# More attention units along block 0, longer DRAM runs for v, k and q, a shorter warm-up, and the last expert's rows turned part by part

## The chip, the cores and the metric

The kernel runs on one core of a Trainium2 chip. The metric is the device time of one execution in microseconds; lower is better. The core's engines have names in the profile: PE (TensorE, matrix products; PEld are its weight loads), DVE (VectorE), ACT (ScalarE), POOL (GpSimd) and SP (SyncE, which issues most DMAs).

## The reference

Three stages follow each other. Inputs are 4 x 8 heads of 576 x 64 q, k and v, and weights.

```python
# 1. attention with random features, for each of 32 heads
phi(x) = exp(h - max(h)) / sqrt(m),  h = x @ omega.T - sum(x * x) / 2
kv = phi(k).T @ v;  z = sum(phi(k))
x = (phi(q) @ kv) / (phi(q) @ z + 1e-6)         # 2304 tokens x 512
# 2. a dense layer
h = x @ w_in                                    # 512 -> 2048
x = (h - tanh(h)) @ w_out                       # 2048 -> 512
# 3. eight experts; each token goes to one, 288 tokens to each
logits = x @ w_gate                             # best pairs (token, expert) first
out[tokens of e] = relu(x[tokens of e] @ w1[e]) @ w2[e]    # 512 -> 1024 -> 512
```

All values are float32. The kernel keeps that precision by splitting operands into a high and a low part and adding three products.

## The kernel before

**Attention** is cut into 72 units. A unit is two heads' worth of a granule of 256 tokens (or of a shared tile of 128). PE projects the granule (line 436, one group of matmuls for two units), DVE takes the negative maxima (`nm`, line 450), ACT the exponentials (`phi`, line 447). For k, PE then adds into `kv` (line 467); for q it transposes `phi` (line 489), multiplies by `kvs` (line 496), and DVE divides (`den`, `xt`, lines 515 to 509).

**The dense layer** runs over six blocks of 384 tokens. A block has 16 chunks of 128 hidden columns. A chunk's first product (`x @ w_in`, lines 611 to 613, twelve matmuls of 384 columns) goes through ACT and DVE (`s`, lines 615 to 638) to the high and low part `gH` and `gL`; its second product (line 658, nine matmuls of 512 columns) adds into three accumulators. Blocks 4 and 5 run together. The weights come in as 32 raw pieces and are prepared on the chip by `weight_ops`: DVE makes `wf` in three passes (lines 341, 343, 345), ACT the high part, DVE or POOL the low part (`lw`, `oL`), which is stored in DRAM and fetched again in each block. In blocks 1 to 3 DVE also multiplies `w_out` with the gate's rows (line 739).

**The experts** follow, one after another, each for 288 tokens in groups of 128, 128 and 32. Its last step multiplies into `py` for four slices d of 128 output columns, copies each to `yT`, transposes them to rows (line 1459), copies these to `mL`, and POOL scatters them (line 1463).

**The order** of the work is not written by hand. Each step is handed to a planner (`Plan`) with a due time `plan.at`, a cost for each engine that may do it, and the buffers that it reads and writes. The planner walks through the steps by its own account of the engines' times, gives each the engine that ends it first, and so fixes one order per engine before the kernel runs; on the chip each engine follows its list strictly. The numbers at the end of `tile_kernel` set the due times: the first 18 units come before block 0 (`NEARLY`), and `along` says how many of the other 54 are spread along each of the blocks 0 to 4:

```python
along = [16, 14, 14, 10, 0]
starts, steps = [T_MLP], []
due = [4.0 + T_UNIT * i for i in range(NEARLY)]
for j, n in enumerate(along):
    steps.append((SB * (1.6 if j == 4 else 1.0) + SU * n) / NF)
    starts.append(starts[j] + NF * steps[j])
    due += [starts[j] + DUE0 + i * (NF * steps[j] - DUE1) / max(n, 1) for i in range(n)]
```

Where the planner sees PE idle for long, it adds short products of ones (`spare`, line 1489) in the stages up to the last weight. The kernel opens with fifteen such products of 512 columns (`warm`, line 1480). In the program there is also a general branch for large values, which this input doesn't take.

## Time and profile before

| what | us |
|---|---|
| median of 3 runs | 867.41 |
| fastest and slowest of them | 864.65, 870.2 |
| the profiled execution | 868.87 |
| its span, from the first to the last instruction | 867.1 |

The page of the profile lists each engine's busy time in the span, and cuts the span in slices; the views behind it give the busy time of any stretch, the waits of an engine and its instructions in order of time. Matmuls overlap in their pipeline, so the distance from one start to the next tells more than the duration of one.

### The profile page before, as it was taken

To read this page: it belongs to the slowest core of one execution; us is meant where nothing else is said; L and a number is where in the kernel's file an instruction comes from. 1 tells how busy PE (TensorE), PEld (TensorE's weight loads), DVE (VectorE), ACT (ScalarE), POOL (GpSimd) and SP (SyncE) were. 2 spreads that over 40 slices of the span, in tenths; PEclk is the share of its full clock that TensorE was granted. 3 is DMA by queue.
4 is the path that set the end of the run, shared out by engine and by line. 5 is a ranking of instruction groups with operands and counts; after the bars stand their busy time and mean duration, and the time that the engine had idled before them with its cause. 6 is when DMAs were issued, how large, how long until landed. Compare 5 with 4: busy or idle time off the path is not lost. (4 is left out here: it accounts for less than half of the span.)

```text
span 867.1 us, 17421 instructions
## 1 busy us (share of the span) xinstructions
PE 839.3 (97%) x6126; PEld 750.9 (87%) x6126; DVE 651.8 (75%) x1906; ACT 470.5 (54%) x1024; POOL 272.5 (31%) x292
## 2 busy tenths in 40 slices
PE   7998999999999999999999999999999999999995
PEld 5988888898888888788988996777999999999995
DVE  6979999778777888878878867445878878876720
ACT  4966564655457554565558864013565555554721
POOL 2131343433353345344423334010042142142211
PEclk9989999999999999999999999999999999999998
DMA  8979877977557665743459884668879879779600
GB/s 258 337 261 286 275 250 236 313 257 241 147 178 226 189 207 161 233 141 113 122 191 320 290 300 144 186 219 267 250 221 299 249 211 301 250 193 343 225 28 28
DMA packets 103790, 193.95 MB, mean 224 GB/s; under 512 B 28305, under 2 KB 42257, under 8 KB 103698
## 3 DMA queue, kind: packets, MB, share of 16 engines
q1 hardware_dynamic: 97586, 172.80, 60.5%
q0 software_dynamic: 5664, 18.88, 9.0%
q8 instruction: 49, 0.80, 0.4%
q10 hardware_dynamic: 448, 1.11, 0.4%
q14 instruction: 43, 0.35, 0.1%
HBM read 149.64 MB, written 33.69 MB: 211 GB/s over the span
## 5 line engine op out<-in xcount | busy, mean ns | idle before, releaser
L305 POOL TENSOR_TENSOR gL<-s,gH 128x384 fp32r<-128x384 f32 x68 | 80.0, 1178 | 172.9 <-ACT gH L300 163.7
L611 PE MATMUL bk<-xH,wi 128*128 128x384 f32 x332 | 118.3, 356 | 4.6 <-ACT phi L447 2.7
L739 DVE SCALAR_TENSOR_TENSOR lw<-wf,raw 128x512 f32<-128x512 f32 x128 | 108.9, 850 | 5.3 <-POOL wf L736 2.6
L612 PE MATMUL bk<-xL,wi 128*128 128x384 f32 x332 | 112.1, 338 | 0.0
L613 PE MATMUL bk<-xH,iL 128*128 128x384 f32 x332 | 112.1, 338 | 0.0
L658 PE MATMUL acc<-wo,gL 128*128 128x512 f32 x282 | 111.4, 396 | 0.0
L658 PE MATMUL acc<-wo,gH 128*128 128x512 f32 x240 | 98.8, 412 | 0.0
L658 PE MATMUL acc<-oL,gH 128*128 128x512 f32 x240 | 95.1, 396 | 0.9 <-DVE oL L305 0.8
L447 ACT ACTIVATE phi<-bk,nm 128x128 f32<-128x128 f32 x268 | 75.8, 384 | 32.9 <-DVE nm L450 32.6
L736 POOL TENSOR_TENSOR wf<-oL,wo 128x512 f32<-128x512 f32 x48 | 66.7, 1390 | 38.7 <-DMA oL<-low_wo 36.3
L611 PEld LDWEIGHTS bk<-xH,wi 128*128 128x128 f32 x332 | 63.0, 190 | 11.9 <-ACT phi L447 3.4
L636 DVE SCALAR_TENSOR_TENSOR s<-s,bk 128x384 f32<-128x384 f32 x83 | 45.4, 549 | 33.2 <-ACT s L635 32.8
L615 ACT ACTIVATE s<-bk 128x384 f32<-128x384 f32 x80 | 39.2, 490 | 55.1 <-PE bk L613 49.2
L300 ACT ACTIVATE gH<-s 128x384 fp32r<-128x384 f32 x80 | 42.0, 525 | 46.2 <-DVE s L638 28.1
L612 PEld LDWEIGHTS bk<-xL,wi 128*128 128x128 f32 x332 | 63.1, 190 | 2.8
L658 PEld LDWEIGHTS acc<-wo,gL 128*128 128x128 f32 x282 | 52.9, 188 | 12.3 <-POOL gL L305 0.5
L613 PEld LDWEIGHTS bk<-xH,iL 128*128 128x128 f32 x332 | 62.9, 189 | 0.0
L638 DVE SCALAR_TENSOR_TENSOR s<-s,s 128x384 f32<-128x384 f32 x80 | 55.4, 693 | 0.9
L635 ACT ACTIVATE s<-s,qbias 128x384 f32<-128x384 f32 x80 | 49.3, 616 | 6.3 <-DVE gL L305 1.9
L658 PEld LDWEIGHTS acc<-oL,gH 128*128 128x128 f32 x240 | 45.2, 188 | 7.4 <-DVE oL L305 1.6
L658 PEld LDWEIGHTS acc<-wo,gH 128*128 128x128 f32 x240 | 45.2, 188 | 6.8 <-issue 1.0
L450 DVE TENSOR_REDUCE nm<-bk 128x4 f32<-128x512 f32 (+1 forms) x74 | 45.7, 633 | 6.8 <-PE bk L436 6.2
(413 smaller groups left out, 2320.4 us busy)
## 6 DMA issues: line engine op xcount, KB each, us to landing
r_wraw<-in_moe_w_dram SPq DMA_DIRECT2D x50, 512.0 KB, 5.3
iL<-low_wi SPq DMA_DIRECT2D x80, 256.0 KB, 3.2
oL<-low_wo SPq DMA_DIRECT2D x78, 256.0 KB, 3.1
raw<-in_moe_w_out_dram SPq DMA_DIRECT2D x32, 512.0 KB, 4.3
raw<-in_moe_w_in_dram SPq DMA_DIRECT2D x30, 512.0 KB, 5.2
s_wraw<-in_moe_w_dram SPq DMA_DIRECT2D x14, 512.0 KB, 5.8
dw<-in_moe_w_dram SPq DMA_DIRECT2D x13, 512.0 KB, 5.3
w1l<-dw SPq DMA_DIRECT2D x13, 512.0 KB, 3.0
```

The costliest lines, as they stand in the source:

```text
L305: (nc.gpsimd if e == POOL else nc.vector).tensor_tensor(out, in_, high.bitcast(F32), op=OP.subtract)
L447: nc.scalar.activation(ph.t[:, i0 + i, :], pj.t[:, i * M:(i + 1) * M], AF.Exp, bias=nmx.t[:, i0 + i:i0 + i + 1])
L450: plan.op(DVE, 0.1 + 0.125 * n, lambda e, pj=pj, i0=i0, n=n: V.tensor_reduce(nmx.t[:, i0:i0 + n], pj.t[:, :n * M].rearrange("p (i m) -> p ...
L611: nc.tensor.matmul(ph(), piece(iH, c), xH.t[:, c, :], start=(c == 0), stop=False)
L612: nc.tensor.matmul(ph(), piece(iH, c), xL.t[:, c, :], start=False, stop=False)
L613: nc.tensor.matmul(ph(), piece(iL, c), xH.t[:, c, :], start=False, stop=(c == NC - 1))
L635: plan.op(ACT, 0.52, lambda e: nc.scalar.activation(s.t, ut(), AF.Square, bias=qbias), r=[u], w=[s], lag=2.8)
L636: plan.op(DVE, 0.52, lambda e: V.scalar_tensor_tensor(s.t, s.t, QD, ph(), op0=OP.add, op1=OP.mult), r=[p, s], w=[s], lag=3.4)
L638: plan.op(DVE, 0.65, lambda e: V.scalar_tensor_tensor(s.t, s.t, QC, ut(), op0=OP.mult, op1=OP.mult), r=[u, s], w=[s], lag=4.0)
L658: nc.tensor.matmul(acc[t].t, (gL if k == 2 else gH).t[:, c], (oL if k == 1 else oH).t, start=(f == 0 and k == 0), stop=(f == end and k == ...
L736: plan.op(POOL, 1.45, lambda e: nc.gpsimd.tensor_tensor(w.t, lo.t.bitcast(F32), wo[:, f, :].bitcast(F32), op=OP.add), r=[lo, wbuf["wo", f] ...
L739: x_reads.append(plan.op(DVE, 0.9, lambda e, i=i: nc.vector.scalar_tensor_tensor(scratch.t.bitcast(F32), w.t, 1.0, half(rows[i // 2], i % ...
```

## The change

The number of units along blocks 0 to 3 becomes 25, 8, 11 and 10; still 54 in all. The times around them change as well: unit and weight due times, and how far ahead x and the low parts are asked for. The planner starts its engines at about a microsecond, takes 300 instead of 280 bytes per ns for DMA, and adds fillers for shorter gaps in the first 25 us. The host lays v out with its column of ones and in the order of the tiles, so that one DMA loads a granule in runs of 2 KB per partition (it was one or two DMAs in pieces of 64 floats, and a memset on POOL); k and q are laid out so that a granule is one run per partition. `omega` comes twice as tall from the host and takes one DMA. The two constants for ACT no longer hold up the projections. One raw weight instead of two is loaded over ACT's queue. The warm-up has seven products. For the last expert the slices are transposed as they come, into one bank for each group of tokens; the last slice is copied in three parts.

```diff
-        self.free = dict.fromkeys(("PE", "ACT", "DVE", "POOL", "SP", "-"), 0.0)
+        self.free = {"PE": 1.6, "ACT": 0.9, "DVE": 1.5, "POOL": 1.2, "SP": 0.9, "-": 0.0}
...
-            if e == "PE" and self.fill and t - self.free[e] > 0.9:
+            if e == "PE" and self.fill and t - self.free[e] > (0.5 if t < 25.0 else 0.9):
...
-                self.dma = max(self.dma, end) + o.nbytes / 280e3
+                self.dma = max(self.dma, end) + o.nbytes / 300e3
...
-        for i in range(2):
-            plan.op(ACT, 0.6, lambda e, i=i: nc.scalar.dma_start(omT[i * D:(i + 1) * D, :], omega), w=[bT], nbytes=P * D * 4)
+        plan.op(ACT, 0.6, lambda e: nc.scalar.dma_start(omT, omega), w=[bT], nbytes=P * M * 4)
...
-            plan.op(ACT, 0.8, lambda e, x=x: nc.scalar.activation(x, x, AF.Copy), w=[bT])
+            plan.op(ACT, 0.8, lambda e, x=x: nc.scalar.activation(x, x, AF.Copy), w=[bBias])
...
-        first = kind == "wi" and f < 2 and not masked
+        first = kind == "wi" and f < 1 and not masked
...
-            plan.op(POOL, 0.04, lambda e: nc.gpsimd.memset(t.t[:, :n, :, D:], 1.0), w=[t], lag=-6.0)
-            for i in range(n):
-                plan.op(SP, 0.47, lambda e, i=i: nc.sync.dma_start(
-                    t.t[:, i, :, :D], v[(tile + i) * P:(tile + i + 1) * P, hh * HH * D:(hh + 1) * HH * D].rearrange(
-                        "p (h d) -> p h d", d=D)), w=[t], lag=-5.0, nbytes=P * HH * D * 4)
+            W = HH * (D + 1)
+            plan.op(SP, 0.47, lambda e: nc.sync.dma_start(
+                t.t.rearrange("p i h d -> p (i h d)")[:, :n * W], v[b // 2, hh, :, tile % 9 * W:(tile % 9 + n) * W]),
+                w=[t], lag=-5.0, nbytes=P * W * 4 * n)
...
-            t.t[:, :, :n * P], src[nm][b // 2, hh * HH * D:(hh + 1) * HH * D, c0:c0 + n * P].rearrange(
-                "(a p) n -> p a n", p=P)), w=[t], lag=-6.0, nbytes=P * HH * D * 4 * n)
+            t.t.rearrange("p a n -> p (a n)")[:, :2 * n * P], src[nm][b // 2, hh, :, 2 * c0:2 * (c0 + n * P)]),
+            w=[t], lag=-6.0, nbytes=P * HH * D * 4 * n)
...
-    LAG2, LEADX, LEADI, LEADO = 10.35, 14.35, 8.14, 3.98
+    LAG2, LEADX, LEADI, LEADO = 10.35, 12.18, 8.65, 5.9
...
-                        plan.at = max(x_due[i * TPB + t] + 11.86, start[j - 1] + LEADX)
+                        plan.at = max(x_due[i * TPB + t] + 15.38, start[j - 1] + LEADX)
...
+    def end_rows(p, d, py, yT):
+
+        if not d:
+            tails[:] = [(Buf(bank3), Buf(mLr), []) for _ in range(NG)]
+        ends = d == NC - 1
+        cp = None
+        if not ends:
+            plan.op({ACT: 0.3, DVE: 0.37}, 0, lambda e: copy(e, yT.t, py.t[:, :CAP]), r=[py], w=[yT])
+            plan.at += 1.0
+        for g in range(NG):
+            (po, yo, done), n, ix = tails[g], GN[g], idxs[p][g][0]
+            cols = slice(g * GS, g * GS + n)
+            if ends:
+                cp = plan.op((ACT, DVE, ACT)[g], 0.2, lambda e, cols=cols: copy(e, yT.t[:, cols], py.t[:, cols]),
+                             r=[py], wp=[yT])
+            done.append(plan.op(PE, 0.11, lambda e, po=po, n=n, cols=cols: nc.tensor.transpose(
+                po.t[:n, d * P:(d + 1) * P], yT.t[:, cols], ident), rp=[yT], wp=[po],
+                after=([cp] if ends else [yT.writers[-1]]) + done[-1:]))
+            if d >= NC - 2:
+                part = slice(0, d * P + P) if not ends else slice(d * P, DM)
+                w = part.stop - part.start
+                plan.op((ACT, DVE, ACT)[g], 0.1 + 0.001 * w, lambda e, po=po, yo=yo, n=n, part=part: copy(
+                    e, yo.t[:n, part].bitcast(F32), po.t[:n, part]), rp=[po], wp=[yo], after=done[-1:])
+            if ends:
+                plan.op(POOL, 1.1, lambda e, g=g, yo=yo, ix=ix: scatter(g, yo, ix), r=[yo, ix], late=3.5)
...
+            if p == E - 1:
+                end_rows(p, d, py, yT)
+                continue
...
-        for i in range(15):
+        for i in range(7):
             nc.tensor.matmul(idle.t, onev.to_broadcast([P, P]), onev.to_broadcast([P, DM]), start=True, stop=True)
...
-    T_UNIT, T_MLP, DUE0, DUE1 = 2.23, 60.95, 7.39, 19.25
+    T_UNIT, T_MLP, DUE0, DUE1 = 2.31, 60.95, 7.04, 19.25
...
-    SB, SU = 39.84, 2.29
-    along = [16, 14, 14, 10, 0]
+    SB, SU = 39.84, 2.36
+    along = [25, 8, 11, 10, 0]
...
-    WI0, WI1, WO0 = 3.84, 2.4, -13.4
+    WI0, WI1, WO0 = 4.16, 1.93, -6.82
```

DVE at the start of the kernel, before: `wf` are passes over a raw weight, `nm` the maxima of a unit.

```order
L315 TENSOR_SCALAR omT<-omT 128x128
L341 TENSOR_SCALAR wf_215<-raw_187 128x512
L343 SCALAR_TENSOR_TENSOR wf_215<-raw_187,wf_215 128x512
L450 TENSOR_REDUCE nm_230<-bk_205 128x4
L450 TENSOR_REDUCE nm_232<-bk_206 128x4
L345 SCALAR_TENSOR_TENSOR wf_215<-raw_187,wf_215 128x512
```

The same place now:

```order
L315 TENSOR_SCALAR omT<-omT 128x128
L451 TENSOR_REDUCE nm_201<-bk_191 128x4
L451 TENSOR_REDUCE nm_205<-bk_192 128x4
L341 TENSOR_SCALAR wf_212<-raw_164 128x512
L343 SCALAR_TENSOR_TENSOR wf_212<-raw_164,wf_212 128x512
L345 SCALAR_TENSOR_TENSOR wf_212<-raw_164,wf_212 128x512
```

The first two maxima moved ahead of the first weight.

DVE in the middle of block 0, before, from the ninth chunk's polynomial (the `s` that reads a bank `bk`) on:

```order
L636 SCALAR_TENSOR_TENSOR s_1467<-s_1467,bk_1360 128x384
L343 SCALAR_TENSOR_TENSOR wf_1475<-raw_1394,wf_1475 128x512
L638 SCALAR_TENSOR_TENSOR s_1467<-s_1467,s_1462 128x384
L345 SCALAR_TENSOR_TENSOR wf_1475<-raw_1394,wf_1475 128x512
L450 TENSOR_REDUCE nm_1519<-bk_1486 128x4
L636 SCALAR_TENSOR_TENSOR s_1512<-s_1512,bk_1416 128x384
```

Now, from the ninth chunk on:

```order
L637 SCALAR_TENSOR_TENSOR s_1454<-s_1454,bk_1402 128x384
L305 TENSOR_TENSOR gL_1475<-s_1184,gH_1464 128x384
L341 TENSOR_SCALAR wf_1486<-raw_1357 128x512
L639 SCALAR_TENSOR_TENSOR s_1454<-s_1454,s_1444 128x384
L343 SCALAR_TENSOR_TENSOR wf_1486<-raw_1357,wf_1486 128x512
L305 TENSOR_TENSOR xL_850<-bk_1467,xH_841 128x4x128
L345 SCALAR_TENSOR_TENSOR wf_1486<-raw_1357,wf_1486 128x512
L516 TENSOR_SCALAR den_1528<-bk_1507 128x4
L518 RECIPROCAL den_1528<-den_1528 128x4
L510 TENSOR_TENSOR xt_1532<-bk_1507,den_1528 128x2x64
L510 TENSOR_TENSOR xt_1536<-bk_1507,den_1528 128x2x64
L341 TENSOR_SCALAR wf_1541<-raw_1436 128x512
```

Before, the tenth chunk's polynomial came five rows behind the ninth's; now twenty-five rows lie between, work of units (`den`, `xt`, `nm`), of weights (`wf`, `oL`) and of the next block's x (`xL`).

PE at the end of the last expert, before (`yT` are the four slices, the last product of the kernel is the first row here):

```order
L1449 MATMUL bd_17105<-s_hH_17044,s_ewL_16843 128x288
L1459 MATMUL bd_17134<-ident,s_yT_17064 128x128
L1459 MATMUL bd_17134<-ident,s_yT_17082 128x128
L1459 MATMUL bd_17134<-ident,s_yT_17109 128x128
L1459 MATMUL bd_17134<-ident,s_yT_17132 128x128
L1459 MATMUL be_17139<-ident,s_yT_17064 128x128
```

PE now, some twenty products before the last one, with the third slice:

```order
L1487 MATMUL bd_17105<-s_hH_16915,s_ewL_16726 128x288
L1396 MATMUL bd_17060<-ident,s_yT_17109 128x128
L1396 MATMUL be_17062<-ident,s_yT_17109 128x128
L1396 MATMUL be_17064<-ident,s_yT_17109 32x128
L1485 MATMUL bd_17105<-s_hH_16932,wi 128x288
```

Three transposes of each of the first three slices now stand between products; only the last slice's three follow the last product.

## Rows read from the trace of the kernel before

**Rows 1.** The page: busy time of each engine, share of the span, instructions.

```profile
...
PE 839.3 (97%) x6126; PEld 750.9 (87%) x6126; DVE 651.8 (75%) x1906; ACT 470.5 (54%) x1024; POOL 272.5 (31%) x292
...
```

**Rows 2.** Busy time by stretch; columns in the first line here.

```profile
...
core 0: us, PE busy (x) PEld busy (x) DVE busy (x) ACT busy (x) POOL busy (x), PEclk, DMA share, GB/s
8.73:49.84 41.11, 36.59 (x362) 33.19 (x363) 38.82 (x87) 33.49 (x105) 10.78 (x13) 0.96 1.04 330
49.84:147.50 97.66, 92.77 (x605) 82.64 (x606) 88.34 (x161) 58.41 (x145) 30.68 (x29) 0.98 0.80 256
8.73:147.50 138.77, 129.35 (x967) 115.82 (x968) 127.16 (x247) 91.90 (x249) 41.46 (x42) 0.98 0.87 278
147.50:246.21 98.71, 98.66 (x637) 87.21 (x637) 75.62 (x183) 53.17 (x130) 41.77 (x52) 1.00 0.72 228
246.21:342.79 96.58, 96.58 (x660) 85.65 (x659) 79.33 (x194) 56.27 (x136) 40.68 (x33) 1.00 0.64 202
46.80:53.60 6.80, 6.24 (x26) 5.62 (x23) 4.87 (x9) 5.00 (x15) 1.27 (x1) 0.50 0.59 221
100.00:140.00 40.00, 38.11 (x224) 32.68 (x223) 37.86 (x65) 23.54 (x55) 16.34 (x14) 1.00 0.75 248
...
```

**Rows 3.** Waits of DVE, 8.73 to 147.5: in total, times, longest.

```profile
...
DVE s L636 <- ACT s L635: 4.3, 5, 2.4
DVE wf L341 <- DMA raw<-in_moe_w_in_dram: 3.4, 1, 3.4
...
```

**Rows 4.** Timeline of the start: start us, us, engine, line, operation.

```profile
...
1.65 5.47 PE L1480 MATMUL bk<-onev 128*128 128x512 bf16 x15 [1.65 <-DVE onev L251]
...
5.12 0.23 DVE L315 TENSOR_SCALAR omT<-omT 128x128 f32<-128x128 f32 x1 [3.58 <-DMA omT<-in_omega_dram]
...
5.86 0.76 PEld L1480 LDWEIGHTS <-onev 128*128 128x128 bf16 x4 [0.25 <-issue]
...
7.05 1.16 PE L436 MATMUL bk<-omT,ld 64*128 64x128 f32 x16
...
8.73 0.43 DVE L341 TENSOR_SCALAR wf<-raw 128x512 uint32<-128x512 uint32 x1 [3.39 <-DMA raw<-in_moe_w_in_dram]
```

**Rows 5.** DMA issues: count, KB each, median us from issue to landing.

```profile
...
v<-in_v_dram SPq DMA_DIRECT2D x36, 128.0 KB, 4.6
...
ld<-in_k_dram SPq DMA_DIRECT2D x16, 256.0 KB, 5.0
...
```

**Rows 6.** Timeline of PE, 55.8 to 60 and 100 to 101.

```profile
...
55.84 1.89 PE L467 MATMUL kv<-v,phi 128*128 128x65 f32 x16
57.67 2.06 PE L436 MATMUL bk<-omT,ld 64*128 64x128 f32 x32
...
100.16 0.40 PE L658 MATMUL acc<-wo,gL 128*128 128x512 f32 x1
100.39 0.39 PE L658 MATMUL acc<-wo,gH 128*128 128x512 f32 x1
...
```

**Rows 7.** Timeline of the tail.

```profile
...
855.26 0.30 PE L1449 MATMUL bd<-s_hH,s_ewL 128*128 128x288 f32 x1
...
855.65 0.41 ACT L300 ACTIVATE s_yT<-bd 128x288 f32<-128x288 f32 x1 [2.77 <-PE bd L1449]
...
856.28 0.60 PE L1459 MATMUL be<-ident,s_yT 128*128 128x128 f32 x4
856.48 0.60 ACT L300 ACTIVATE mL<-bd 128x512 f32<-128x512 f32 x1 [0.42 <-PE bd L1459]
...
857.36 0.98 POOL L1463 DMA_INDIRECT out_dram<-mL,r_ix  x1 [22.87 <-ACT mL L300]
...
```

**Rows 8.** Groups of DVE, 8.73 to 147.5: count, busy us, mean ns.

```profile
...
L450 DVE TENSOR_REDUCE nm<-bk 128x4 f32<-128x512 f32 x26 | 17.2, 682 | 1.5 <-PE bk L436 1.1 <-PE rx L436 0.3
...
L509 DVE TENSOR_TENSOR xt<-bk,den 128x128 f32<-128x128 f32 x24 | 6.1, 283 | 0.2
...
L305 DVE TENSOR_TENSOR gL<-s,gH 128x384 fp32r<-128x384 f32 x4 | 2.4, 612 | 1.1 <-ACT gH L300 1.1
...
```

44 lines of the change are left out of this document (28 added, 16 removed).

## The prediction

> **What bounds the kernel now.** I read the page first: TensorE (PE) is busy for 839.3 of 867.1 us [rows 1], so the time is PE's work plus what PE loses, and only stages where it loses can pay. Then I cut the span at the first products `x @ w_in` of each block and asked for the busy time of every engine in each stretch [rows 2]. The reader is to compare PE and VectorE (DVE) line by line. From 147.50 on, through blocks 1 and 2, PE has no idle time at all (98.66 of 98.71, 96.58 of 96.58) while DVE is busy for four fifths: what leaves these blocks shortens them one for one, and what enters lengthens them. Block 0, 49.84 to 147.50, is different: PE idles 97.66 - 92.77 = 4.9 us, and DVE is busy 88.34 of 97.66 us; from 100 to 140 it is busy 37.86 of 40. The stretch before it, 8.73 to 49.84, is DVE's too (38.82 of 41.11). So from 8.73 to 147.50 DVE sets the pace: it prepares the weights (three or four passes each), takes the maxima of the attention units and does the polynomial of each chunk, in a fixed order. The waits of DVE in that stretch [rows 3] are few: 4.3 us for ScalarE and 3.4 for one weight's DMA lead them. One more loss stands in rows 2: from 46.80 to 53.60 the granted clock is 0.50, that is 1.2 instead of 2.4 GHz, with PE busy for 6.24 us; that costs up to 3.1 us. The last stage, the experts, is PE's alone until the tail.
>
> My durations are of one profiled execution of 868.87 us (span 867.1); the median is 867.41, within 0.2%, and I apply the differences to the median.
>
> **Start of the kernel.** Before, fifteen warm-up products run from 1.65 for 5.47 us, and the first projections follow at 7.05 [rows 4]; `omT` is scaled at 5.12 to 5.35, so they waited for the warm-up alone. Eleven of their weight loads lie between 1.65 and 5.86, about 0.42 us apart, and the last four take 0.76 us together: the clock came up near 5.8. Seven products end at 1.65 + 7 x 0.42 = 4.6. The projections can then start at 5.4 (`omT`), or near 5.9 if the first k granule takes the median 5.0 us from its issue at 0.87 [rows 5]; the 16 matmuls take 1.16 us at the clock of before, up to twice that at the lower one. DVE's first maxima now stand ahead of the first weight (the order shows it), so DVE starts work at 7.3 to 8.7 instead of 8.73. **Worth 0 to 1.4 us of DVE's time.**
>
> Here a rule speaks against the change. The row shows a clock that rose after four microseconds of unbroken products; the shorter warm-up ends before that moment. The Trainium skill (TensorE: Matmul & The Clock Gate, What's actually happening) says that the throttled state is the default and that activity releases it; by that, a warm-up that stops early can leave the projections slow. The trace agrees that the kernel starts slow. I take it as a rival below.
>
> **The loads.** v came in pieces of 64 floats, 256 bytes, in 36 issues of 128 KB that landed after 4.6 us, hardly sooner than 256 KB of k after 5.0 [rows 5]. Now a granule of v is one issue of 2 KB runs, and k and q are single runs too. The DMA engines are at 1.04 from 8.73 to 49.84 [rows 2], so this frees transfer time. What it is worth is bounded: DVE's order is fixed and it idles only 41.11 - 38.82 = 2.3 us there, so **0 to 2.3 us**; I take it inside the middle of the next sum. The 36 memsets of the ones column leave GpSimd, which nobody waits for, and are costed at nothing. The Trainium skill (DMA: Bandwidth & Descriptors, Specifications) asks for at least 512 bytes for line rate; if DMA were the bound, the gain would be larger, but the waits say that it is not.
>
> **The units along the blocks.** This is the large term. Between the first product of block 0 and that of block 1 PE's order gains 36 rows of projections (two matmuls each; 32 matmuls take 2.06 us [rows 6], 0.058 each once the drain of the last, some 0.2, is taken off: 0.115 a row), 28 rows of `kv` and 8 of numerators (two matmuls each; 16 take 1.89 us, 0.112 each without the drain: 0.224 a row), 8 transposes of 0.11 [rows 7] and 9 products of the second kind at 0.23 [rows 6]: 4.1 + 6.3 + 1.8 + 0.9 + 2.1 = 15.2 us. Another 4 rows of `kv` (0.9 us) go ahead of block 0. Blocks 1 and 2 lose the same rows, 16.1 us together; block 3 keeps its rows. As PE never idles in blocks 1 and 2, they get 16.1 us shorter.
>
> What does block 0 get longer? DVE must say. Up to the first product of block 1 its order gains 8 maxima of 128x512 at 0.68, 2 of half that, 4 `gL` at 0.61 and 4 `xt` at 0.28 [rows 8], which is 5.5 + 0.7 + 2.4 + 1.1 = 9.7; five short rows and two passes of line 739 come against two `oL` that leave, an estimate of 1.6 us from the same rows: 11.3 us on top of 127.16 [rows 2], 138.5 us. If DVE keeps its share of before, 127.16 / 138.77 = 91.6%, and starts at 8.73, block 0 ends at 8.73 + 138.5 / 0.916 = 159.9, 12.4 later, and 16.1 are given back: **-3.7**. If it starts at 7.3 and reaches the 94.65% of 100 to 140, it ends at 153.6, 6.1 later: -10.0. But PE cannot give more than it lost: 4.9 idle and 3.1 of slow clock, **-8.0**. I take the middle of -3.7 and -8.0, **-5.9**, since nothing in the rows says whether the new mix of work between the chunks lets DVE wait less; the order shows long stretches of unit work between two chunks, which keep both engines supplied but also hold a chunk's polynomial up.
>
> The new lead times (low parts of `w_out` asked for 1.9 us earlier, `w_in` 0.5) move transfers by little in stages where DMA is at 0.5 to 0.8; the planner's own rate and start constants matter only through the order. The extra fillers (36 more matmuls of 128 columns) run where the planner saw PE idle; they would cost up to 36 x 0.06 = 2.1 us if it isn't (at the 0.058 of the projections, which have as many columns). Half of them stand in the early stage, where PE waits anyway; I leave them out of the sum.
>
> **The tail.** Before, the last product starts at 855.26, the last `yT` (288 columns) takes ACT 0.41 us from 855.65, the transposes wait for it, the first `mL` is copied from 856.48 in 0.60 and the first scatter is issued at 857.36 [rows 7], 2.10 after the last product. Now the last copies are of 128 columns; by the line through 0.41 (288) and 0.60 (512) these take 0.27 each, so the first scatter can be issued 0.14 + 0.33 = 0.47 earlier, behind the last product. But nine transposes that came after it now stand in front of it, between the products, at 0.11 each (four in 0.44 from 856.28): 1.0 us, and PE is dense there. Three of them lay in PE's wait before, but that wait costs the chain nothing. The three scatters follow one another on GpSimd as before. **+0.5**, between -0.5 (the transposes slip into gaps) and +0.6.
>
> **Sum:** 867.4 - 5.9 + 0.5 = **862.0 us**.
>
> **The rivals.** (1) DVE falls behind in block 0, the slower side. The place: chunks of block 0 whose polynomial stands behind unit work and weights; 4.3 us of DVE's waits are for ScalarE already [rows 3], which gets ten more groups of exponentials there. It decides when DVE's share from 8.73 falls below 138.5 / (147.5 + 16.1 - 8.73) = 89.4%. At 87% block 0 ends at 167.9: +20.4 - 16.1 + 0.5 = +4.8, 872.2. Against it: ScalarE is busy for 58.41 of 97.66 us there [rows 2], and the weights still to come are the same. (2) All fits: PE's idle time and the slow clock vanish, and the early loads give their 2 us: 867.4 - 8.0 - 2.0 + 0.5 = 857.9. For it: DVE did reach 94.65% for 40 us. (3) The warm-up is too short, and the first projections and sums run at 1.2 GHz. If the low clock lasts as long as the stretch in rows 2 (6.8 us) and PE is half busy, it costs up to 3 us: 865.0. Against: DVE, not PE, is the bound there.
>
> **How the numbers follow.** Forecast 0.5 (862.0, within 859 to 865), rival 1 0.2, rival 2 0.2, rival 3 0.1. 1% is 8.7 us, about what a measurement of this kernel can tell from no change (its runs spread from 864.65 to 870.2). Below 858.7: two thirds of rival 2 and a fifth of the forecast, 0.24. Above 876.1: the far end of rival 1, 0.06. The range has rival 2 with 5 us of spread below, and rival 1 above: 853 to 873.
>
> **What would show it.** Block 0's first product should stay near 49.8 and block 1's come 8 to 12 us later than 147.5; blocks 1 and 2 should shrink by some 11 and 5 us with PE still fully busy; DVE's share up to block 1 should be 92 to 95%; the tail should show three transposes among the last products. The prediction is wrong if block 0's first product moves by over 3 us, which would mean that DVE's work ahead of it was not the bound, or if PE begins to idle in blocks 1 to 3.

## The result, and the profile after

The changed kernel takes 875.46 us (median of 16 runs, 867.4 to 882.57) against 866.82 us for the kernel before (16 runs, 863.8 to 873.8): a ratio of 1.0084, 95% interval 1.0055 to 1.0114. The ratio leaves out two executions of the changed kernel that lie over 1.5% above its fastest (880.57 and 882.57), so it is smaller than the quotient of the medians. The forecast was 862.0, between 853 and 873, and the time lies above that range. The profiled execution takes 873.41 us, its span is 871.6.

The page of the changed kernel answers to [rows 1]. PE's busy time rose by 7.6 us with 28 more instructions (36 more fillers, 8 fewer warm-up products).

```profile
...
PE 846.9 (97%) x6154; PEld 759.2 (87%) x6154; DVE 660.9 (76%) x1913; ACT 469.5 (54%) x1028; POOL 265.5 (30%) x266
...
```

The busy time by stretch answers to [rows 2]. Its stretches run from DVE's first maxima to block 0's first product, through a part of that in which the granted clock was at its lower level, and then through blocks 0, 1 and 2; the last is from block 4 to the end.

```profile
...
core 0: us, PE busy (x) PEld busy (x) DVE busy (x) ACT busy (x) POOL busy (x), PEclk, DMA share, GB/s
7.21:54.91 47.70, 43.25 (x389) 40.04 (x389) 42.27 (x90) 34.64 (x108) 9.89 (x8) 0.86 0.87 290
21.37:31.61 10.24, 10.24 (x65) 9.49 (x65) 6.80 (x12) 5.39 (x18) 1.28 (x1) 0.50 1.02 372
54.91:169.35 114.44, 112.08 (x786) 99.24 (x785) 97.83 (x184) 71.88 (x186) 35.08 (x26) 0.98 0.75 250
169.35:256.29 86.94, 86.94 (x533) 77.08 (x533) 68.98 (x177) 44.24 (x103) 29.91 (x37) 1.00 0.67 213
256.29:347.44 91.15, 91.15 (x595) 80.12 (x594) 78.84 (x178) 49.57 (x118) 40.64 (x31) 1.00 0.66 208
439.80:871.60 431.80, 415.94 (x3223) 378.52 (x3221) 290.75 (x1076) 214.96 (x386) 108.90 (x129) 0.99 0.71 226
...
```

For that last stretch, the kernel before:

```profile
...
437.30:867.10 429.80, 415.49 (x3223) 378.16 (x3221) 292.62 (x1082) 214.81 (x382) 106.51 (x126) 0.99 0.71 227
...
```

The reader is to see four things. Block 0's first product came at 54.91, 5.1 us later than before. In the early stage the mean granted clock is 0.86 (it was 0.96), and from 21.37 to 31.61 it is 0.50, 1.2 GHz, and so it is again from 52.09 on; before, there was no such stretch ahead of 46.78. Block 0 takes 114.44 instead of 97.66 us, and blocks 1 and 2 take 178.09 instead of 195.29: what they gave back, 17.2, block 0 took, 16.8. And the stretch from block 4 to the end takes 431.80 instead of 429.80. By stages the span thus grew by 5.07 ahead of block 0, shrank by 2.57 from there to block 4 (439.80 against 437.30), and grew by 2.00 behind: 4.5 together, 871.6 against 867.1. The medians are 8.6 apart because the profiled execution lies 2.05 below its median here, and that of before 2.05 above.

The timeline at the start answers to [rows 4]: start, us, engine, line, operation.

```profile
...
2.00 3.17 PE L1514 MATMUL bk<-onev 128*128 128x512 bf16 x7 [2.00 <-DVE onev L251]
...
3.49 0.23 DVE L315 TENSOR_SCALAR omT<-omT 128x128 f32<-128x128 f32 x1 [1.60 <-DMA omT<-in_omega_dram]
...
5.09 2.08 PE L437 MATMUL bk<-omT,ld 64*128 64x128 f32 x16
...
7.21 1.29 DVE L451 TENSOR_REDUCE nm<-bk 128x4 f32<-128x512 f32 x2 [3.49 <-PE bk L437]
...
```

Seven warm-up products end earlier than fifteen did, and the projections start at 5.09. They take 2.08 us, nearly twice [rows 4]'s 1.16, so they ran at 1.2 GHz. DVE still starts at 7.21 instead of 8.73. That was foreseen. What was not stands in the timeline around 28:

```profile
...
25.77 1.02 DVE L451 TENSOR_REDUCE nm<-bk 128x2 f32<-128x256 f32 x2
...
28.00 0.58 PE L437 MATMUL bk<-omT,ld 64*128 64x128 f32 x1
...
30.01 1.11 PE L490 MATMUL rx<-ident,phi 128*128 128x128 f32 x4
...
30.16 0.69 DVE L451 TENSOR_REDUCE nm<-bk 128x4 f32<-128x512 f32 x1 [3.38 <-issue]
...
```

DVE waits 3.38 us for a projection. The releaser reads "issue", but the matmuls that it needs run right there, the first in 0.58 us; at 2.4 GHz the first of such a group takes 0.37 (b_num's timeline below, at 10.90). PE is busy throughout the slow stretch (10.24 of 10.24 us), DVE for 6.80: with the clock at 1.2 GHz PE is the bound, and DVE waits.

The tail answers to [rows 7]:

```profile
...
860.26 0.29 PE L1487 MATMUL bd<-s_hH,s_ewL 128*128 128x288 f32 x1
860.59 0.28 ACT L300 ACTIVATE s_yT<-bd 128x128 f32<-128x128 f32 x1 [1.73 <-PE bd L1487]
...
861.32 0.27 ACT L300 ACTIVATE mL<-bd 128x128 f32<-128x128 f32 x1
...
861.87 0.97 POOL L1372 DMA_INDIRECT out_dram<-mL,r_ix  x1 [23.32 <-ACT mL L300]
...
```

From the last product to the first scatter it is 1.61 us; before, it was 2.10.

### The profile page after: what moved, and what is told of

Read it like the earlier page. It is cut to its first block, busy times and chain, and to the rows that moved or that the text cites. A ratio compares the mean times of both kernels' runs of the same rounds, so it can differ in the third digit from the quotient of the medians.

```text
span 871.6 us, 17405 instructions
## 1 busy us (share of the span) xinstructions
PE 846.9 (97%) x6154; PEld 759.2 (87%) x6154; DVE 660.9 (76%) x1913; ACT 469.5 (54%) x1028; POOL 265.5 (30%) x266
## 5 line engine op out<-in xcount | busy, mean ns | idle before, releaser
L305 POOL TENSOR_TENSOR gL<-s,gH 128x384 fp32r<-128x384 f32 x58 | 68.6, 1183 | 154.2 <-ACT gH L300 154.2
L448 ACT ACTIVATE phi<-bk,nm 128x128 f32<-128x128 f32 x272 | 77.8, 378 | 30.2 <-DVE nm L451 29.9
L737 POOL TENSOR_TENSOR wf<-oL,wo 128x512 f32<-128x512 f32 x48 | 66.6, 1389 | 55.8 <-DMA oL<-low_wo 49.0
L639 DVE SCALAR_TENSOR_TENSOR s<-s,s 128x384 f32<-128x384 f32 x80 | 62.3, 778 | 1.2
```

Source lines behind the costliest of these rows:

```text
L305: (nc.gpsimd if e == POOL else nc.vector).tensor_tensor(out, in_, high.bitcast(F32), op=OP.subtract)
L448: nc.scalar.activation(ph.t[:, i0 + i, :], pj.t[:, i * M:(i + 1) * M], AF.Exp, bias=nmx.t[:, i0 + i:i0 + i + 1])
L639: plan.op(DVE, 0.65, lambda e: V.scalar_tensor_tensor(s.t, s.t, QC, ut(), op0=OP.mult, op1=OP.mult), r=[u, s], w=[s], lag=4.0)
L737: plan.op(POOL, 1.45, lambda e: nc.gpsimd.tensor_tensor(w.t, lo.t.bitcast(F32), wo[:, f, :].bitcast(F32), op=OP.add), r=[lo, wbuf["wo", f] ...
```

## The experiments

Each kernel ran beside the kernel before on the same chip; the ratio is to that. "First" is the start of block 0's first product in the profiled execution, the next columns are the time from there to block 4's first product and from there to the end of the span, and the last is the stretch that begins ahead of 45 us, if any, in which the granted clock was 0.50 after it had first come up. Sixteen of the twenty lose the clock once more near block 0's first product, between 46.8 and 59.2; the exceptions are b_warm7, a_dense_oldnum, b_phase and a_best_num. The kernel before had medians of 866.4, 871.9, 867.0, 865.7 and 866.4 us in the five sets; in the second, marked *, the kernel before took some 5 us longer, so that its times by stage are not to be compared with the others.

| kernel | ratio, 95% interval | first | to block 4 | to the end | early low clock |
|---|---|---|---|---|---|
| before | | 49.84 | 387.46 | 429.80 | none |
| changed | 1.0084, 1.0055 to 1.0114 | 54.91 | 384.89 | 431.80 | 21.37 to 31.61 |
| a_warm15 | 1.0133, 1.0097 to 1.0169 | 54.27 | 387.45 | 433.78 | 44.75 to 48.16 |
| b_warm7 | 1.0027, 1.0003 to 1.0050 | 49.82 | 383.42 | 429.36 | none, but up only near 14 |
| a_oldnum | 1.0066, 1.0043 to 1.0090 | 55.03 | 384.52 | 433.25 | 21.13 to 31.37 |
| a_oldtail | 1.0082, 1.0052 to 1.0112 | 55.20 | 384.08 | 434.02 | 18.84 to 32.49 |
| a_280 * | 1.0072, 1.0042 to 1.0101 | 53.65 | 394.19 | 436.26 | 20.34 to 33.99 |
| b_num * | 1.0031, 1.0001 to 1.0061 | 56.74 | 385.20 | 435.76 | 11.82 to 25.48 |
| lay * | 1.0064, 1.0035 to 1.0093 | 50.49 | 390.36 | 435.65 | none |
| a_dense * | 1.0049, 1.0022 to 1.0076 | 51.55 | 388.26 | 437.49 | none |
| lay_same | 1.0029, 1.0006 to 1.0052 | 51.33 | 383.68 | 428.49 | none |
| b_dense | 1.0019, 0.9987 to 1.0051 | 52.21 | 386.46 | 430.53 | 11.37 to 14.79 |
| a_dense_oldnum | 1.0047, 1.0018 to 1.0075 | 48.72 | 382.46 | 433.52 | none |
| b_edits | 1.0043, 1.0016 to 1.0071 | 54.74 | 388.39 | 431.77 | 21.61 to 31.85 |
| b_phase | 1.0007, 0.9979 to 1.0036 | 50.44 | 384.44 | 432.22 | 11.54 to 14.95 |
| a_late | 1.0101, 1.0056 to 1.0146 | 55.04 | 385.40 | 430.26 | 19.11 to 32.77 |
| b_num_late | 1.0019, 0.9994 to 1.0044 | 50.45 | 389.05 | 429.20 | none |
| a_best | 0.9991, 0.9962 to 1.0020 | 51.62 | 381.78 | 428.40 | none |
| a_best_tail | 0.9990, 0.9964 to 1.0016 | 56.86 | 383.53 | 431.21 | 20.66 to 34.31 |
| a_best_num | 1.0011, 0.9983 to 1.0040 | 48.79 | 384.61 | 430.30 | none |

**The warm-up.** The first theory was C: the shorter warm-up lets the clock fall, and that costs the time. a_warm15 is the changed kernel with fifteen products, b_warm7 the kernel before with seven.

```diff
-        for i in range(7):
+        for i in range(15):
```

a_warm15: 

> The changed kernel with fifteen warm-up products instead of seven; nothing else moves in any engine's order. Theory C (the short warm-up lets the granted clock fall): no 1.2 GHz stretch between 20 and 33 us, VectorE's idle time of 3.4 us near 27 to 30 is gone, block 0's first product comes at 50 to 52 instead of 54.9, and the time falls by 3 to 5 us, to about the kernel before (ratio 0.998 to 1.004). Rival S (the early stage's new order is too sparse for TensorE by itself: it was busy for only 1.40 of 2.5 us from 17.5 to 20): the low stretch stays, the first projections come 1 to 2 us later, and the time stays at 1.006 to 1.011 of before.

b_warm7: 

> The kernel before with seven warm-up products instead of fifteen; nothing else moves. Theory C: a low stretch of about 10 us appears before 35 us, block 0's first product moves from 49.8 to 52 to 55, and the time rises by 3 to 5 us (ratio 1.003 to 1.006). Rival S: no new low stretch, block 0's first product stays at 49 to 50, ratio 0.998 to 1.001.

Both missed. In the changed kernel with the longer warm-up the stretch from 21 to 32 is gone, and the kernel was no faster all the same (1.0133 against 1.0084, with intervals that overlap). DVE's order in the changed kernel begins with the maxima, so it waits out the longer warm-up, here in its timeline:

```profile
...
9.09 1.29 DVE L451 TENSOR_REDUCE nm<-bk 128x4 f32<-128x512 f32 x2 [5.47 <-PE bk L437]
...
```

It starts 1.9 us later than with seven. And the clock fell later instead, twice, as the busy time by stretch shows:

```profile
...
20.00:22.50 2.50, 1.40 (x15) 1.21 (x13) 2.50 (x5) 2.50 (x11) 1.26 (x1) 1.00 0.96 327
44.75:48.16 3.41, 3.41 (x24) 3.07 (x24) 3.15 (x11) 1.45 (x5) 0.39 (x1) 0.50 0.52 185
51.58:54.99 3.41, 3.41 (x16) 3.41 (x17) 3.13 (x5) 2.58 (x8) 1.27 (x1) 0.50 0.51 194
...
```

In the kernel before, seven products cost 0.27%, with an interval that begins just above 1, and block 0's first product came where it had been:

```profile
...
8.70:49.82 41.12, 36.94 (x362) 33.85 (x362) 38.01 (x86) 33.59 (x105) 9.64 (x12) 1.00 0.97 298
49.82:144.66 94.84, 91.23 (x605) 81.12 (x606) 88.58 (x161) 58.88 (x145) 33.38 (x30) 1.00 0.86 276
...
```

The clock column reads 1.00 from 8.70 on, but this trace has no record of the clock ahead of its first rise, and the matmuls tell when that was. The same projections take longer up to 12 us than behind 14:

```profile
...
5.84 2.08 PE L436 MATMUL bk<-omT,ld 64*128 64x128 f32 x16 [1.03 <-DVE omT L315]
...
11.75 0.42 PE L436 MATMUL bk<-omT,ld 64*128 64x128 f32 x1
...
14.80 0.27 PE L436 MATMUL bk<-omT,ld 64*128 64x128 f32 x1
...
```

So with seven products the clock came up only near 14 (before, near 5.8), and the first product came no later: 49.82 against 49.84. The kernel before had a low stretch of its own from 46.78, and what that hides of the late rise isn't known. Fifteen products don't save the time in the other order. The run also shows what the kernel before would do without its own low stretch at 46.78: block 0 takes 94.84 instead of 97.66.

**The parts one by one.** a_oldnum has the numbers of before (units along the blocks, due and lead times), a_oldtail the tail of before, a_280 the planner's rate of before.

```diff
-    along = [25, 8, 11, 10, 0]
+    along = [16, 14, 14, 10, 0]
...
-            if p == E - 1:
-                end_rows(p, d, py, yT)
-                continue
...
-                self.dma = max(self.dma, end) + o.nbytes / 300e3
+                self.dma = max(self.dma, end) + o.nbytes / 280e3
```

a_oldnum: 

> The changed kernel with the numbers of the order as before: 16, 14, 14 and 10 units along blocks 0 to 3, and the due and lead times of before. Layout, short warm-up, planner's start values and tail stay changed. Theory N (the numbers cost more in block 0 than they give back later): block 0 takes about 98 us again instead of 114, and the time falls below the changed kernel by 2 to 4 us (ratio 1.003 to 1.006, the rest being the low clock). Theory C alone, with numbers that are worth what the prediction gave them: the time rises to 1.012 to 1.017.

a_oldtail: 

> The changed kernel with the last expert's rows turned after the last slice, as before. By the prediction's own sum the new tail costs 0.5 us, between a gain of 0.5 and a loss of 0.6, so the time falls by 0.5 (ratio 1.008 against the 1.0084 of the change). Rival L (the tail and what its planning moves among the experts cost the 2.3 us that the changed kernel loses after block 5 begins): the time falls by 2 us (ratio 1.006).

a_280: 

> The changed kernel with the planner's DMA rate at 280 bytes per ns again and nothing else undone; by its order VectorE has one copy and one pass of a weight less, and PE four rows of kv less, ahead of block 0's first product. Theory O (the order that the new rate brings puts the extra work there, and with fifteen warm-up products it stood at 54.3 all the same): block 0's first product comes 2 to 4 us earlier, at 51 to 53, and the time falls by 2 to 4 us (ratio 1.004 to 1.006). Rival D (VectorE starts late or the low clock holds it, whatever the order): it stays at 54 to 55, ratio 1.007 to 1.010.

Each of the three still loses over 0.6%, and each has the early low stretch and its first product at 53.65 or later. The old numbers gave back 0.18% and the old tail 0.02%, both within the intervals. What they have in common is the early stage and, as the column to the end tells, 3.4 and 4.2 us more behind block 4 in a_oldnum and a_oldtail, even where the tail is the old one (3.41 us of low clock near 540 are in each).

b_num is the kernel before with the new numbers alone, lay the layout with the two small edits of its loads, in the order that the planner then makes.

b_num: 

> The kernel before with the new numbers alone: 25, 8, 11 and 10 units along blocks 0 to 3 and the new due and lead times. The early stage's order is that of before up to block 0's first product. Theory Z (block 0 gets longer by all the work that it takes over and idles as before, so that the numbers are worth nothing): block 0 takes 113 to 115 us, block 4 begins within 1.5 us of 437.3, ratio 0.998 to 1.002. The prediction's term: block 0 grows by 8 to 12 us only, block 4 begins 4 to 8 us earlier, ratio 0.991 to 0.996.

lay: 

> The new layout of v, k, q and omega alone, with the loads that go with it (one raw weight over ACT's queue, ACT's constants not ahead of the projections); fifteen warm-up products, numbers, planner's start values, rate and tail as before. The prediction's term for the loads: 0 to 2.3 us earlier at block 0's first product, which then comes at 47.5 to 50, ratio 0.997 to 1.000. Rival O (shorter loads change the planned order of the early stage, and that costs more than the transfers give): first product at 51 or later, ratio 1.002 to 1.006.

b_num's early stage has the order of before and fifteen warm-up products, and yet its first product came at 56.74. Its PE timeline and its busy time show how the clock was lost:

```profile
...
6.64 1.16 PE L436 MATMUL bk<-omT,ld 64*128 64x128 f32 x16
10.90 0.37 PE L436 MATMUL bk<-omT,ld 64*128 64x128 f32 x1 [3.09 <-DMA ld<-in_k_dram]
...
```

```profile
...
7.50:10.00 2.50, 0.31 (x6) 0.11 (x3) 1.12 (x3) 0.00 (x0) 0.00 (x0) 1.00 1.12 332
11.82:25.48 13.66, 13.66 (x91) 12.98 (x88) 8.88 (x14) 7.00 (x24) 2.71 (x4) 0.50 0.74 213
...
```

A k granule landed late, PE had 0.31 us of work in 2.5, and at 11.82 the clock fell for 13.66 us. PE in the kernel before waits there too (0.71 us of work from 7.50 to 10.00) and kept its clock. This can happen to any of these kernels; the question is how often, and at what price. lay took 103.02 us for block 0, with 7.8 us of low clock in it, and kept its early clock. It also carries an order of the experts of its own (below), so its 0.64% is not one cause.

**Fillers.** a_dense leaves the changed kernel's order alone and adds filler products wherever the planner saw a gap of PE ahead of 62 us, 77 instead of 28 before block 0; b_dense does it to the kernel before (44 instead of 10).

```diff
-            if e == "PE" and self.fill and t - self.free[e] > (0.5 if t < 25.0 else 0.9):
-                self.fill(min(0.4 * (t - self.free[e]), 1.0))
+            if e == "PE" and self.fill and t - self.free[e] > (0.25 if t < 62.0 else 0.9):
+                self.fill(min((0.8 if t < 62.0 else 0.4) * (t - self.free[e]), 1.6))
```

a_dense: 

> The changed kernel with 77 instead of 28 filler products ahead of block 0's first product, where the planner saw gaps of PE; all other instructions stand as in the changed kernel. Theory C (low clock): if it keeps the clock up from 20 to 60, VectorE's 3.4 us of idle time near 27 to 30 go, block 0's first product comes at 51 to 52.5, and the time falls by 3 to 5 us (ratio 1.002 to 1.005). Rival O (the order and VectorE's own work set the stage): the clock stays up but block 0's first product comes at 53.5 or later, and the time stays at 1.007 to 1.010.

b_dense: 

> The kernel before with 44 instead of 10 filler products ahead of block 0's first product; no other instruction moves. Theory C (PE's gaps let the clock fall, and that costs time in most runs): the low stretch near 46 to 54 goes, the mean granted clock of the runs rises by 0.002 to 0.004, ratio 0.996 to 0.999. Rival F (the fillers only delay): block 0's first product later than 51, ratio 1.001 to 1.004.

a_dense_oldnum (also with the numbers of before): 

> The changed kernel with the numbers of before and with the dense fillers. If the two causes are separate, their gains add up (the old numbers gave 0.2%, the fillers 0.35%): ratio 1.001 to 1.004. Rival: both act through the same wait of VectorE in the early stage, ratio 1.005 to 1.008.

a_dense did what theory C said: no low stretch ahead of 48, the first product at 51.55, 0.35% gained, the least of the gain that was expected, with intervals that overlap. In the kernel before, whose early clock held without them in the profiled execution, the fillers gave nothing, and the low stretch near 46 to 54 that they were to remove stayed (48.92 to 55.75). a_dense_oldnum, at 1.0047, fell between its two expectations; its first product came at 48.72, 1.1 us earlier than in the kernel before. Up to there its order is the changed kernel's, fillers apart. So the order of the changed early stage is not slow in itself; the rival O, that it holds more work of DVE, falls.

**The layout and two small edits.** lay_same gives the kernel before the new layout with the order of every engine untouched. b_edits gives it only the two edits that went along: one raw weight instead of two on ACT's queue, and ACT's constants not ahead of the projections.

```diff
-        first = kind == "wi" and f < 2 and not masked
+        first = kind == "wi" and f < 1 and not masked
...
-            plan.op(ACT, 0.8, lambda e, x=x: nc.scalar.activation(x, x, AF.Copy), w=[bT])
+            plan.op(ACT, 0.8, lambda e, x=x: nc.scalar.activation(x, x, AF.Copy), w=[bBias])
```

lay_same: 

> The kernel before with v, k and q laid out in DRAM as in the change and every engine's order as before (v still one DMA for each tile, now of 1040 bytes per partition; GpSimd's memsets go to a spare tile; omega as before). Theory P (the layout run alone lost through the order that the planner made of it): ratio 0.996 to 1.001, and block 0's first product at 48 to 50. Rival D (the transfers themselves cost, say by coming sooner and taking bandwidth from others): ratio 1.004 to 1.007.

b_edits: 

> The kernel before with only the two small edits that went with the layout: one raw weight instead of two over ACT's queue, and ACT's two constants no longer ahead of the projections. By the planner's order VectorE has one first pass of a weight, one low part and one copy more ahead of block 0's first product, but not a whole weight. Theory P2 (these edits make the order that costs): ratio 1.003 to 1.007. Rival: they are harmless, ratio 0.998 to 1.002, and the order that costs comes of the shorter issue of v's loads.

The layout alone gains nothing; at 1.0029 it fell between the two expectations, and a gain lies outside its interval. The two edits alone, with fifteen warm-up products and an early order of their own, come out in the profiled execution as the changed kernel did: a low stretch from 21.61 to 31.85, the first product at 54.74. Their busy time by stretch:

```profile
...
17.50:20.00 2.50, 1.21 (x17) 1.02 (x15) 2.50 (x5) 1.74 (x6) 0.28 (x2) 1.00 1.05 341
21.61:31.85 10.24, 10.24 (x65) 9.38 (x64) 4.85 (x9) 6.91 (x23) 1.86 (x3) 0.50 1.07 341
...
```

PE had 1.21 us of work from 17.50 to 20.00. In the changed kernel it had 1.40:

```profile
...
17.50:20.00 2.50, 1.40 (x18) 1.21 (x17) 2.50 (x5) 2.31 (x8) 1.27 (x1) 1.00 1.01 331
...
```

**The experts' order.** The planner rounds its times to steps of 0.03 us before it compares due times. Where its clock starts at the experts depends on all that it planned before, so an edit ahead of the experts can deal them a new order. b_phase gives the kernel before the changed kernel's start value there and changes nothing else; a_late gives the changed kernel the value and rate of before.

```diff
-    now = max(plan.free.values())
+    now = 1472.338213333387
```

b_phase: 

> The kernel before, with nothing moved up to the experts; there the planner's clock starts from the changed kernel's value (1472.338 instead of 1474.697 us in its own account), which alters only how its times are rounded to steps of 0.03 us, and with that the order of the experts' work (of VectorE's 899 instructions there half stand in the same sequence as before). Theory X (part of the change's loss is a worse order of the experts that no part of the change was about): the stretch from block 4 to the end takes 431.5 to 434 us instead of 429 to 430, ratio 1.002 to 1.005. Rival: the orders are worth the same, ratio 0.999 to 1.001.

a_late: 

> The changed kernel with the experts' order of before: from the experts on the planner's clock starts at the value that it has in the kernel before, and its DMA rate is 280 again; the new tail stays, and nothing moves ahead of the experts. Theory X: the stretch from block 4 to the end falls by 2 to 3.5 us to 429 to 430.5, ratio 1.004 to 1.006. Rival: it stays near 432 because of the new tail, ratio 1.007 to 1.010.

From block 4 to the end:

```profile
...
434.88:867.10 432.22, 417.76 (x3223) 379.78 (x3221) 290.71 (x1079) 215.12 (x382) 104.40 (x127) 0.99 0.70 225
...
```

```profile
...
440.44:870.70 430.26, 416.20 (x3223) 379.76 (x3221) 291.71 (x1078) 214.37 (x384) 108.93 (x129) 0.99 0.70 226
...
```

The traces go as theory X said, 2.4 us more and 1.5 less, though each of the two has 3.41 us of low clock near 535 to 541, where the kernel before and the changed one have none; so 2.4 is at the most what the order cost, and 1.5 at the least what it gave. The times don't tell it: b_phase's interval holds 1 and X's lower end, and a_late's six runs came out at 1.0101, with mean granted clocks of 0.977 to 0.985, where fourteen of the changed kernel's sixteen have 0.985 to 0.996. The lower clock covers it. With fillers it shows: a_dense_oldnum and a_best_tail differ in nothing but the experts' order, and have 1.0047 (1.0018 to 1.0075) and 0.9990 (0.9964 to 1.0016), each against the kernel before on its own chip. From block 4 to the end they took, in this order:

```profile
...
431.18:864.70 433.52, 416.86 (x3223) 379.50 (x3221) 290.17 (x1078) 214.00 (x386) 109.22 (x129) 0.99 0.70 225
...
```

```profile
...
7.21:56.86 49.65, 46.38 (x438) 43.24 (x436) 41.17 (x90) 35.20 (x109) 10.92 (x8) 0.84 0.83 279
20.66:34.31 13.65, 13.65 (x92) 12.70 (x93) 8.78 (x15) 7.41 (x27) 1.27 (x1) 0.50 0.94 318
440.39:871.60 431.21, 417.68 (x3223) 380.61 (x3221) 292.55 (x1080) 214.57 (x384) 109.78 (x129) 0.98 0.70 226
...
```

The second has the lower clock in this stretch and is still 2.3 us shorter.

**The numbers and the tail without the rest.** b_num_late is b_num with the experts' order held. a_best has the changed kernel's layout, edits, rate and warm-up with dense fillers, the experts' order of before, and the old numbers and tail; a_best_tail and a_best_num put the new tail and the new numbers back.

b_num_late: 

> The kernel before with the new numbers alone, as once before, but with the experts' order held at that of before, so that the numbers' own worth is seen. Theory Z (block 0 gets longer by the work that it takes over, blocks 1 and 2 shorter by as much): ratio 0.998 to 1.002, and from block 0's first product to block 4 it takes 383 to 387 us. The prediction's term: ratio 0.992 to 0.996.

a_best: 

> A candidate: the changed kernel with the numbers and the tail of before, dense fillers ahead of block 0, and the experts' order of before; the layout, the short warm-up and the planner's rate of 300 up to the experts stay. Theories C and X together: what is left of the change's loss is gone, and the early loads' gain is seen, ratio 0.995 to 1.000. Rival (the changed early order costs by itself, fillers or not): 1.001 to 1.004.

a_best_tail: 

> The candidate (the changed kernel with the numbers of before, dense fillers and the experts' order of before) with the new tail again, so that the tail's own worth is seen where nothing else differs. The prediction's term: 0.5 us more, ratio 0.999 to 1.001; the stretch from the last product to the end 0.4 to 0.6 us shorter than the 11.8 of before. Rival: the new tail costs more among the experts, ratio 1.002 or more.

a_best_num: 

> The candidate with the new numbers (25, 8, 11, 10 units and their due times) and the tail of before. Theory Z (the numbers are worth nothing or cost up to 0.3%): ratio 0.999 to 1.003; from block 0's first product to block 4 it takes 383 to 387 us. The prediction's term, with the clock held up: ratio 0.991 to 0.995.

a_best is as fast as the kernel before, 0.92% below the changed one; no version beat the kernel before measurably. The tail is worth nothing (0.9990 against 0.9991). The numbers cost 0.2% in a_best, 0.19% in the kernel before and 0.18% in the changed kernel; each lies within the noise (b_num's 0.31% just outside it, with an experts' order of its own), but all agree in sign, and the forecast's 0.68% gain lies outside b_num_late's interval. a_best_num and a_best_tail also carry the same early work in the same order up to block 0 and show what the clock is worth there. The first line of the fence below is a_best_num's early stage, the second its block 0; above stand a_best_tail's early stage and its low stretch.

```profile
...
7.21:48.79 41.58, 38.31 (x423) 35.68 (x421) 38.56 (x89) 33.89 (x108) 9.43 (x7) 1.00 0.95 328
48.79:161.80 113.01, 110.75 (x799) 98.09 (x797) 97.91 (x185) 72.27 (x188) 35.86 (x26) 1.00 0.76 252
...
```

Between the two first products lie 8.07 us, but the stretch of 13.65 us isn't all of it. In a_best_num the clock was up before the projections, so that DVE's maxima start 0.9 us sooner, and a_best_tail's clock was low again from 54.79 on. A copy of DVE that follows the low stretch (`kvs`) tells the parts. First a_best_num:

```profile
...
6.31 1.29 DVE L452 TENSOR_REDUCE nm<-bk 128x4 f32<-128x512 f32 x2 [2.65 <-PE bk L438]
...
29.20 0.42 DVE L303 COPY kvs<-kv 128x260 f32<-128x260 f32 x1
...
```

Then a_dense, whose maxima start at 7.20 and which has the same order and no low stretch before the copy:

```profile
...
30.09 0.42 DVE L302 COPY kvs<-kv 128x260 f32<-128x260 f32 x1
...
```

Then a_best_tail:

```profile
...
7.19 1.29 DVE L452 TENSOR_REDUCE nm<-bk 128x4 f32<-128x512 f32 x2 [3.51 <-PE bk L438]
...
36.24 0.43 DVE L303 COPY kvs<-kv 128x260 f32<-128x260 f32 x1
...
```

So the slow projections cost 0.9 us, **the low stretch 6.15 us** (36.24 against 30.09), and the end of the stage 1.0. In the changed kernel the copy stands at 33.83: 3.7 us for its stretch of 10.24, and 6.1 us in all (54.91 against 48.79). Block 0 of a_best, to be laid beside a_best_num's, and its last stretch:

```profile
...
51.62:147.57 95.95, 94.24 (x651) 84.23 (x648) 89.19 (x165) 59.13 (x143) 31.53 (x25) 1.00 0.80 268
433.40:861.80 428.40, 415.85 (x3223) 379.83 (x3221) 288.43 (x1077) 214.77 (x382) 109.99 (x129) 0.99 0.71 227
...
```

**The time at an equal clock.** In the five sets every run lists its mean granted clock, and within a kernel the time follows it: over 345 runs, 0.66 us for each thousandth of the clock (0.59 to 0.73 by set). An estimate by this rate takes the clock out of each kernel's mean distance to the kernel before beside it. Of the changed kernel's loss 1.4 to 2.2 us are then its lower clock (0.9884 on average, the kernel before 0.9905 to 0.9917). The new numbers cost 2.4 us in b_num_late, and 2.5 from a_best to a_best_num, with standard errors of some 0.4 and 0.6; so their cost is clear of nothing, which in the plain times it was not. The experts' order cost 1.8 us in b_phase and 4.2 from a_best_tail to a_dense_oldnum. The layout in the order of before costs nothing (lay_same, -0.2), and a_best comes out 1.0 us below the kernel before.

## Why the prediction was wrong

**The step that weighed most** is the term of the units, -5.9 us, which at an equal clock came out as some +2.5 (above). **The step that failed first** is the early stage: "Block 0's first product should stay near 49.8", and the third rival's price, "up to 3 us", with its "Against: DVE, not PE, is the bound there". DVE is the bound at 2.4 GHz. At 1.2 GHz PE is (10.24 of 10.24 us busy while DVE did 6.80), and the stretch of 13.65 us in a_best_tail cost 6.15, that of 10.24 in the changed kernel 3.7. With the slow projections and the end of the stage the low clock cost the changed kernel 6.1 us there, twice the price that I gave. I worked that price out from [rows 2]'s 6.80 us stretch with PE half busy, though PE's row there says 6.24 of 6.80. The first product moved by 5.07, over the 3 us that I had named as a sign of being wrong.

The reason that I gave for the low clock falls short too. The edits that I left without a cost in the sum, one raw weight on ACT's queue and the constants off the projections' path, brought the stretch with fifteen warm-up products as well (b_edits's profiled execution). They reorder the units so that PE has 1.2 to 1.4 us of work in the 2.5 us ahead of 20, and the clock fell behind that. Of the profiled executions with the changed early stage and no added fillers (the changed kernel, a_oldnum, a_oldtail, a_late, and a_280 with an order of its own) five of five have a low stretch of 10 to 14 us that begins at 18.8 to 21.4. With dense fillers in that order it is one of five, and among the seven without the edits one of 13.66 us and two of 3.4, and b_warm7's clock came up late. With the edits and fifteen products, b_edits has it, a_warm15 and lay don't. Whether a gap loses the clock is not certain: a_warm15 had 1.40 us of work from 20.00 to 22.50 and kept it, a_best_num had 1.84 and kept it, a_best_tail 1.85 and lost it. So this is a matter of chance for each execution, with odds that, as far as these few show, the order sets, and it spreads the runs: the changed kernel took 867.4 us at a mean clock of 0.996 and 879.2 at 0.985.

The Trainium skill (TensorE: Matmul & The Clock Gate, What's actually happening) calls the throttled state the default, released by activity, and says that the same kernel starts differently from run to run. The traces agree: in the same order the first sixteen projections took 1.19 us in a_best_num and 2.06 in a_best_tail. They show besides that the clock falls again inside a busy kernel, for 13.65 us in a stage where PE had work in nine tenths of the time.

**The units along the blocks** were to gain 5.9 us. Blocks 1 and 2 shrank by 17.2, as the order said (16.1), and DVE's work up to block 1 grew to 42.27 + 97.83 = 140.1 us against the 138.5 worked out. The term that failed is block 0: it was to grow by 8 to 12, and grew by 16.8. With the numbers alone (b_num_late) it grew by 17.3, and blocks 1 and 2 shrank by 14.1 only (165.39 to 346.59, 181.2 us); the rest of the 17.2 came with the change's other edits. I had let the moved work fill the 4.9 us that PE idled and the 3.1 that the low clock cost. Neither is there to be filled. In a_best, block 0 leaves PE idle for 1.7 us, and with the new numbers it takes 17.06 us more, of which PE is busy for 16.51. In the kernel before, the idle time doesn't shrink either; with the numbers alone PE idles 6.11 us in block 0:

```profile
...
50.45:165.39 114.94, 108.83 (x765) 96.98 (x766) 96.91 (x184) 71.97 (x190) 29.47 (x31) 0.98 0.77 247
...
```

The first rival had this outcome: below a DVE share of 89.4% the change loses. From 7.21 to 169.35 the share was 140.1 / 162.14 = 86.4%, and block 0 ended at 169.35, near the rival's 167.9 at 87%. Its reason, chunks whose polynomial stands behind unit work, fits only a part of block 0. From 71.26 to 100.17 DVE is full and PE idles 2.2 us; behind that PE is dense, and DVE has the time:

```profile
...
71.26:100.17 28.91, 26.71 (x198) 22.39 (x196) 27.99 (x50) 17.39 (x44) 13.63 (x9) 1.00 0.97 336
100.17:146.92 46.75, 46.59 (x323) 40.73 (x321) 43.23 (x92) 33.13 (x90) 13.19 (x10) 1.00 0.72 238
...
```

My own row had PE at 92.77 of 97.66 us in block 0, 95% busy; two engines were near full, and I read one of them as the bound.

**The loads** were bounded at 0 to 2.3 us. With the order untouched the layout gained nothing (1.0029), although lay_same's packets under 512 bytes fell from 28,305 to 9,873. The kernel before and lay_same:

```profile
...
DMA packets 103790, 193.95 MB, mean 224 GB/s; under 512 B 28305, under 2 KB 42257, under 8 KB 103698
...
```

```profile
...
DMA packets 84845, 194.02 MB, mean 225 GB/s; under 512 B 9873, under 2 KB 19217, under 8 KB 84754
...
```

The Trainium skill (DMA: Bandwidth & Descriptors, Specifications) asks for 512 bytes for line rate; the runs show that here no time hung on it. With the changed order and the clock up (48.79 and 48.72 against 49.84) start and loads together gave 1.1 us, and the kernel before had 3.06 us of low clock ahead of its first product. DVE started at 6.31 and 6.25 there instead of 8.73. The bound held; what the transfers had in the gain isn't told apart from the start.

**The tail** was right in its parts: from the last product to the first scatter 1.61 us instead of 2.10, 0.49 less where 0.47 was worked out. The net of +0.5 can't be told from 0.

**What the sum lacked** is the experts: their order came out otherwise, though no part of the change was about them, and took 2.0 us more in the profiled execution, with no low clock in that stretch before the last product in either kernel, and 1.8 to 4.2 at an equal clock. I wrote that the planner's constants "matter only through the order" and then looked at the order in blocks 0 to 3 alone.

By stages of the profiled execution: +5.1 from the early low clock net of an earlier start, -2.6 through block 3 (both executions have some 4 us of low clock in block 0; without any, and with the changed early stage, the numbers of before take 382.46 in a_dense_oldnum and the new ones 384.61 in a_best_num), +2.0 from block 4 on. Of the 13.5 us between the forecast and the median, the units make up some 8.4, the lower clock some 2 and the experts' order some 2 to 4, by the estimates at an equal clock. Not settled: why lay's and b_edits' block 0 takes 103 us (7.8 and 4.4 us of it at the low clock), and which stretches of low clock the runs without a profile had.

## What to carry to other kernels

Where PE and the engine ahead of it are both near full, work moved into that stage lengthens it by its whole duration, and idle time of a few per cent isn't a place to put it. In a stage with thin PE work, look at the order for a gap of PE that a small edit opens: what it costs is not the gap but the low clock behind it, which makes PE the bound for ten microseconds or more. Where the clock varies from run to run, set the times beside each run's mean clock before comparing two kernels. Under a planner with rounding or ties, an edit can reorder stages that it isn't about: hold those fixed, or measure them apart, before giving the edit the difference.

## What was not expected of the hardware

A low stretch of 13.65 us in the early stage cost 6.15 us, so that its chance alone moves the time by 0.7%. In b_warm7 the clock came up 8 us later than before, and block 0's first product came at 49.82 instead of 49.84. In the second set the kernel before took from 867.7 us at a mean granted clock of 0.996 to 877.9 at 0.982. And the chips differ: the same kernel had medians of 865.7 to 871.9 us in the five sets, each on another chip.
